# Free convolution streams, earlier key bounds and a transposed last normalization in a kernel of attention beside a long convolution

## The chip, the cores and the metric

The kernel runs on one core of a Trainium2 chip. The core has five engines with queues of their own: TensorE (matrix products into PSUM), VectorE, ScalarE, GpSimd and SyncE, which here only issues DMA transfers; GpSimd issues some too. Work passes between engines by semaphores, and each engine takes its instructions strictly in the order in which the program has them. The metric is the time of one execution on the device in microseconds (us); lower is better.

## The reference

Two independent parts stand side by side in the output (2048 rows, 576 + 576 columns).

Part A is a long convolution. For each of 576 channels a kernel K of 2048 taps is made from 128 complex modes, and the input u is convolved with it causally:

```python
dt = jnp.exp(log_dt)[:, None]
logdA = dt * (A_re + 1j * A_im)
P = jnp.exp(logdA[:, :, None] * l[None, None, :])
K = jnp.einsum("dn,dnl,dn->dl", Cc, P, dt * Bc).real
y = irfft(rfft(u, 2L) * rfft(K, 2L))[:L] + u * Dskip
```

Part B is attention with 32 query heads of width 18 that share one key head and one value head, over 2048 rows:

```python
q = (x @ wq) in 32 heads;  k = x @ wk;  v = x @ wv
p = softmax(q @ k.T * 18 ** -0.5)
out = concat_heads(p @ v) @ wo
```

## The kernel before

**Tiling of part B.** The queries are cut into four chunks c of 512 columns, the heads into 16 pairs, the keys into 16 blocks kb of 128. One *score tile* is the scores of one key block against the 512 queries of two heads (`scores`, two matmuls into one PSUM tile s of 128 x 1024). ScalarE takes the exponential of the tile into P (`exponentials`, one ACTIVATE of about 1.03 us each, 1024 of them). Then `product` multiplies the P of two score tiles (four heads, a group g) by the values and adds them in the PSUM tile o over the 16 key blocks. The value matrix carries columns of ones, so row 18 of every head's 32 rows of o holds the sum by which the head must be divided. Score tiles have three PSUM buffers (NS = 3), and the main loop goes in rounds of three: three score tiles, then products and other work until ScalarE has released the first of the three. P has ten buffers.

Before a group's scores can be made, its queries must be projected (`qproj`, matmuls q), split into two half-precision parts (qh, ql), and given a *shift row* that keeps the exponential in range. The shift comes from a bound: `settle` and `bounds` (lines 371 and 393) make for all query rows the largest key entries (kmx, a matmul into 20 columns, then kmax), and `bound` (line 504) multiplies them with the largest query entries (aw), sums with a small matmul (up), takes the running maximum (un, u) and writes the shift row (sh), which goes to DRAM by a DMA that GpSimd issues. SyncE fetches the complete operand (aug) from DRAM. No query projection but the first begins before `bounded` is set.

When a group is done, o goes to DRAM (od). `normalize` (line 577) fetches the sums, inverts them, stores them (rden), fetches them again spread over 18 rows each (db), and multiplies; `outproj` does the product with wo (op). For the last chunk three quarters of this are done in parts as the groups finish, and `finish` (line 664) does the last group after the last exponential: it inverts the sums where they lie (VectorE, two halves of 256 columns), spreads them over the rows of their head by a matmul with a 0/1 matrix b4 (bc), scales the last o, and adds the product with wo (fin) to the partial result.

**Tiling of part A.** The channels go in 12 groups k of 48. `front(k)` makes the kernel: powers and factors on VectorE and ScalarE (four groups share one set of powers, kept in DRAM), tables of products on VectorE (tab), and matmuls kg that sum the modes (`kgen`); the result ksb goes through DRAM (kd) into another layout kt. `back(k)` transforms the inputs u (matmuls hu, lu) and the kernel kt (hk, lk) by matmuls with a table of cosines and sines, multiplies the spectra on VectorE (pt, acc), and transforms back (iy). There is one buffer kt: `front(k + 1)` holds its finished kernel until `back(k)` has read the former one.

**What sets the order.** The instruction order of TensorE, ScalarE and VectorE is written out by the program itself when it is built. A planner (`main`, `Clock`, `Stream`) keeps modelled clocks of the three engines. Side work is written as generators (streams): `side` (query and output projections), `tail` (bounds), `prep` (normalization) and the convolution's streams. Each stops at points of a kind: "v" (VectorE work may follow), "p" (matmuls may follow), "b" (an activation table is wanted), "w" (it waits for another stream). In every round `fill` asks the streams for work as long as the modelled TensorE has room, and the constants RATE to C12 say how much room, how far ahead VectorE may be and which stream comes first; PLAN sets them anew in 16 stages of 32 steps (a step is two score tiles). Except for the score tiles and o, all matmuls write to one shared PSUM bank (`bank`, tile f): the next user has to wait until VectorE has emptied it.

In the convolution `turn` starts the pair `back(k)` and `front(k + 1)` and starts the next pair when both have ended; among the two, `go` asks the one first that has done less work.

Of the kernel before, what the change touches and what calls it, by code (L numbers as in the profile page):

```python
# [17 lines left out]
P = 128  # L18
# [32 lines left out]
LAST = 576.841  # L51
# [3 lines left out]
    0: dict(RATE=1.86, PACE=1.856, AHEAD=0.729, TOTAL=340.0, GAP=0.359, DEFER=0.395, SLACK=3.285, HEAD=17.08, LEFT=1.086, C1=0.549, C2=0.718, C3=0.83, C4=1.39, C5=0.739, C6=1.059, C7=0.572, C8=0.186, C9=0.382, C10=0.431, C11=24.516, C12=11.926),  # L55
    1: dict(RATE=1.838, AHEAD=0.731, HEAD=10.76, C3=0.633, C4=1.288, C6=0.962, C8=0.227, C11=22.979),
    2: dict(AHEAD=0.937, TOTAL=426.375, SLACK=2.955, HEAD=8.992, LEFT=1.137, C3=0.83, C4=1.267, C6=0.825, C11=24.516),
    3: dict(AHEAD=0.729, TOTAL=340.0, DEFER=0.389, SLACK=3.285, HEAD=13.454, LEFT=1.086, C2=0.563, C6=1.059, C8=0.186),
    4: dict(PACE=1.877, DEFER=0.395, C2=0.718, C3=0.886, C8=0.257, C12=9.229),
    5: dict(DEFER=0.334, C1=0.507, C3=0.973, C9=0.468, C10=0.418),  # L60
    6: dict(C3=0.912, C4=1.331, C5=0.562, C8=0.216, C9=0.573, C12=11.451),
    7: dict(TOTAL=393.142, HEAD=15.028, C1=0.596),
    8: dict(PACE=1.856, C8=0.186, C12=14.796),
    9: dict(GAP=0.311, DEFER=0.395, C1=0.601, C2=0.561, C6=0.861, C9=0.468),
    10: dict(PACE=1.834, HEAD=14.988, C1=0.497, C9=0.382),
    12: dict(TOTAL=300.519, C1=0.607, C2=0.687, C12=11.271),
    13: dict(AHEAD=0.591, TOTAL=393.142, SLACK=2.63, C1=0.65, C5=0.726, C6=1.059, C10=0.39, C12=14.796),
    14: dict(C1=0.533, C2=0.561, C7=0.595, C9=0.379, C12=11.755),
    15: dict(AHEAD=0.503, C3=1.026, C4=1.582, C8=0.194),
# [144 lines left out]
class Attention:  # L214
# [36 lines left out]
    def setup(self, tp, conv):  # L251
# [51 lines left out]
        self.tails = []  # L303
# [67 lines left out]
    def settle(self, conv):  # L371
# [17 lines left out]
        K.t += 1.0  # L389
        K.v = K.t + 2.0  # L390
        K.fill = K.v

    def bounds(self):

        nc, V, K = self.nc, self.V, self.k
        km, spread = self.km, self.spread
        self.bounded = True
        pk = self.bank(20, "kmx")
# [406 lines left out]
    def main(self, conv, flag):  # L805
# [75 lines left out]
        for r in range(0, len(pairs), NS):  # L881
# [22 lines left out]
            if r == 2 * NS:  # L904
                self.bounds()
# [727 lines left out]
```

## Time and profile before

| | us |
|---|---|
| median of 3 runs | 1141.29 (1140.82 to 1143.82) |
| the profiled execution | 1140.67 |
| its span, first to last instruction | 1138.9 |
| first exponential of the main loop | 26.79 |
| end of the last exponential | 1121.02 |
| busy: TensorE, VectorE, ScalarE | 1080.4, 992.7, 998.9 |

The profile names engines PE (TensorE), PEld (TensorE's weight loads), DVE (VectorE), ACT (ScalarE), POOL (GpSimd) and SP (SyncE). A row of a group or of the timeline ends, in square brackets or behind a bar, with the idle time just before it and what ended it. A row of the waits reads: who waited, for whom, total, times, longest. Row counts of fp32 matmuls are twice those of the program, since each is done in two passes. Line numbers are those of the kernel before. Vector operations of many streams share one helper line (137), so groups are told by their tiles: `out<-in`.

### The profile page before, as it was taken

The page shows a single profiled execution, that of the slowest core. Times are in us where ns is not written, and L with a number is a line of the kernel's source. Part 1 is how long each engine was busy: PE and PEld are TensorE (multiplying, and loading weights), DVE is VectorE, ACT ScalarE, POOL GpSimd, SP SyncE. Part 2 cuts the span into 40 slices and gives each one's busy share as a digit, 9 for nine tenths or more (in the row PEclk, how much of TensorE's full clock was granted, in tenths as well). Part 3 has the DMA queues.
Part 4 walks back from the last instruction along what each step waited for, and adds up shares of the span by engine and source line. Part 5 has one row for each costly group of instructions (what it writes and reads, how often), then busy time and mean ns, then how long its engine had stood idle before and what let it go on. Part 6 is the DMA issues. An engine that isn't in the chain of part 4 may idle for free.

```text
span 1138.9 us, 33011 instructions
## 1 busy us (share of the span) xinstructions
PE 1080.4 (95%) x13886; PEld 395.6 (35%) x13886; DVE 992.7 (87%) x1692; ACT 998.9 (88%) x1052; POOL 140.0 (12%) x257
## 2 busy tenths in 40 slices
PE   6999999998998999999999999999989999999997
PEld 2333333333333333323333333333322333433423
DVE  3878998899899898998799899899699799799794
ACT  2878988888997899999898999899999999889993
POOL 4442324122023000000201211000000000000000
PEclk9999999999999999999999999999999999999999
DMA  7432234212222301122202301201222311311201
GB/s 224 146 101 75 64 118 135 63 39 50 84 82 87 95 29 59 50 88 88 89 9 82 106 22 36 97 29 40 68 95 67 99 40 38 97 39 35 72 30 59
DMA packets 59279, 83.37 MB, mean 73 GB/s; under 512 B 14867, under 2 KB 35335, under 8 KB 58613
## 3 DMA queue, kind: packets, MB, share of 16 engines
q1 hardware_dynamic: 47557, 73.24, 20.1%
q0 software_dynamic: 10848, 7.37, 2.6%
q8 instruction: 111, 1.82, 0.7%
q10 hardware_dynamic: 720, 0.58, 0.2%
q14 instruction: 43, 0.35, 0.1%
HBM read 46.59 MB, written 33.85 MB: 71 GB/s over the span
## 4 chain that ended last, share of the span: by engine, by line
PE 59%; DVE 21%; ACT 10%; issue 6%; DMA 3%; POOL 1%; DVEq 0%; SPq 0%; ACTq 0%
PE ops L869 24%; PE s L550 15%; ACT P L561 9%; PE op L211 5%; DVE tab L137 5%; PE kg L1314 3%; DVE ks L137 3%; PE iy L211 3%; PE q L427 2%; DVE acc L137 2%; DVE tt L137 1%; PE hu L211 1%; PE hk L211 1%; DVE pt L137 1%; DMA db<-rden 1%
## 5 line engine op out<-in xcount | busy, mean ns | idle before, releaser
L561 ACT ACTIVATE P<-s 128x1024 f32<-128x1024 f32 x992 | 934.8, 1035 | 97.2 <-PE s L550 94.3
L869 PE MATMUL ops<-P,v_sb 128*32 128x512 f32 x4096 | 509.5, 599 | 3.0 <-DVE o L141 2.8
L550 PE MATMUL s<-aug,kaug 55*128 55x512 f16 x2048 | 307.5, 381 | 23.6 <-ACT P L561 20.8
L550 PEld LDWEIGHTS <-kaug 55*128 55x128 f16 x2048 | 93.2, 94 | 341.6 <-issue 292.9
L869 PEld LDWEIGHTS ops<-P,v_sb 128*32 128x32 f32 x4096 | 118.2, 110 | 162.8 <-issue 131.0
L478 POOL DMA_DIRECT2D qd<-qh x116 | 66.3, 578 | 317.8 <-DVE qh L145 315.2
L427 PE MATMUL q<-x,wq_sb 128*32 128x256 f32 x1360 | 83.6, 382 | 0.3 <-PE s L550 0.3
L211 PE MATMUL op<-wo_sb,oT 126*32 126x288 f32 (+1 forms) x960 | 67.5, 410 | 2.5 <-DVE ob L141 2.5
L1225 POOL MEMSET fr<- 128x192 f32 x24 | 9.9, 497 | 481.6 <-DVE tt L137 242.5
L137 DVE TENSOR_TENSOR tab<-tab,tt 128x576 f32<-128x576 f32 (+1 forms) x72 | 59.0, 820 | 1.5
L137 DVE TENSOR_TENSOR tab<-fr,dif 128x576 f32<-128x576 f32 (+1 forms) x72 | 58.7, 815 | 0.0
L137 DVE TENSOR_TENSOR tt<-fr,sum 128x576 f32<-128x576 f32 (+1 forms) x72 | 58.7, 815 | 0.0
L137 DVE TENSOR_TENSOR tab<-sum,fr 128x576 f32<-128x576 f32 (+1 forms) x72 | 58.6, 814 | 0.0
L137 DVE TENSOR_TENSOR tab<-tab 128x576 f32<-128x576 f32 (+1 forms) x72 | 58.5, 813 | 0.0
L141 DVE COPY ksb<-kg 128x192 f32<-128x192 f32 x48 | 17.3, 360 | 41.5 <-PE kg L1314 41.5
L427 PEld LDWEIGHTS q<-x,wq_sb 128*32 128x32 f32 x1360 | 39.9, 109 | 38.4 <-issue 14.4
L137 DVE TENSOR_TENSOR acc<-acc,pt 128x1728 f32<-128x1728 f32 (+2 forms) x36 | 48.6, 1349 | 0.2
L137 DVE TENSOR_TENSOR pt<-us,ks 128x1728 f32<-128x1728 f32 (+2 forms) x36 | 48.3, 1347 | 0.0
L1314 PE MATMUL kg<-tab 128*32 128x64 f32 x2304 | 41.8, 220 | 5.6 <-DVE tab L137 3.4
L1314 PEld LDWEIGHTS kg<-tab 128*32 128x32 f32 x2304 | 36.5, 110 | 29.6 <-issue 9.8
L559 ACT ACTIVATE P<-s,bias 128x1024 f32<-128x1024 f32 x32 | 33.0, 1115 | 13.4 <-PE s L550 13.4
L137 DVE TENSOR_TENSOR ks<-ks 128x576 f32<-128x576 f32 (+1 forms) x48 | 41.0, 855 | 1.0
(163 smaller groups left out, 1020.9 us busy)
## 6 DMA issues: line engine op xcount, KB each, us to landing
od<-o SPq DMA_DIRECT2D x31, 256.0 KB
aug<-qd SPq DMA_DIRECT2D x124, 55.0 KB
u<-u SPq DMA_DIRECT2D x12, 384.0 KB
kd<-ksb SPq DMA_DIRECT2D x12, 384.0 KB
kt<-kd SPq DMA_DIRECT2D x48, 96.0 KB
outa<-u SPq DMA_DIRECT2D x12, 384.0 KB
pw<-pw SPq DMA_DIRECT2D x8, 528.0 KB
db<-rden SPq DMA_DIRECT2D x16, 252.0 KB
```

Of the source, the lines that this page charges most:

```text
L137: return self.v.tensor_tensor(out, *a, **k)
L141: return self.v.tensor_copy(out, *a, **k)
L211: nc.tensor.matmul(ps[j:e], w[:, j:e], x, start=start, stop=stop, tile_position=(0, j))
L427: nc.tensor.matmul(ps[o, 256 * f:256 * f + 256], w[:, k, i], xt[:, k, x], start=(k == 0), stop=(k == 4), tile_position=(0, 32 * j))
L478: q.dma_start(qd[h:h + n, row + d:row + d + nd, cs], src[i1:i1 + n * nd, :cs.stop - cs.start])
L550: nc.tensor.matmul(ps[:, j, :], self.kaug[r, kb * P:(kb + 1) * P], t[r, :], start=True, stop=True)
L559: nc.scalar.activation(pt, ps, AF.Exp, bias=self.bias, scale=SCALE / QQ)
L561: nc.scalar.activation(pt, ps, AF.Exp, scale=SCALE / QQ)
L869: nc.tensor.matmul(o_ps[32 * j:32 * j + 32, :], self.v[:, kb, :], pts[2 * n + j // 2][:, j % 2, :], start=(kb == 0), stop=(kb == 15), tile ...
L1225: nc.gpsimd.memset(t[:, :, 0:NF:8], one)
L1314: nc.tensor.matmul(ps[32 * g:32 * g + 32, d, :], t[:, :32], t[:, 32:], start=(j == 0), stop=(j == 1), tile_position=(0, 32 * g))
```

## The change

1. **Key bounds.** What `bounds` did in the third round of scores is now done at the end of `settle`, in the first round, directly behind the matmuls that transpose the values. Its PSUM tile comes from the output pool (o) and no longer from the shared bank.
2. **Shift rows.** The tile sh has three buffers where it had one.
3. **Normalization.** While the main loop runs, the multiplication is asked for 7.0 us (model time) behind its fetch, where it was 4.6.
4. **Last sums.** `finish` copies the last o (ScalarE one half, VectorE the other), brings the 4 sums of each query to the partitions with 16 small matmuls, inverts a tile of 128 x 16, and spreads the inverses with 16 matmuls against the identity (id4, loaded behind b4).
5. **Convolution streams.** The pairs are gone. One stream runs all fronts, one all backs. A back waits until the front of its group (first group) or of the group before (all others) has sent its kernel, transforms u, and only then waits for its own kernel. Of two streams that both have VectorE work, the one served last comes first.
6. **Table.** PLAN has 32 stages of 16 steps, other values, and LAST is 618.0 where it was 576.8. The modelled cost of a round of scores is 0.04 us less.

```diff
-LAST = 576.841
+LAST = 618.01458
 PLAN = {
...
+    0: dict(RATE=1.87109, PACE=1.81374, AHEAD=0.81305, TOTAL=379.90864, GAP=0.27563, DEFER=0.50556, SLACK=3.20468, HEAD=12.56556, LEFT=0.69661, C1=0.35905, C2=0.57071, C3=0.95845, C4=1.22733, C5=0.56371, C6=0.74724, C7=0.51086, C8=0.17113, C9=0.53612, C10=0.37123, C11=37.75411, C12=17.28614),
...
+LAG = (0, -1)
@@ settle: @@
-        K.t += 1.0
-        K.v = K.t + 2.0
-        K.fill = K.v
-
-    def bounds(self):
...
         self.bounded = True
-        pk = self.bank(20, "kmx")
+        pk = self.ps_o.tile([P, CT], F32, tag="o", name="kmx")[:, :20]
...
-        K.pe(1.5)
-        K.v = max(K.v, K.t + 0.5)
-        K.fill = K.v + 0.25
+        K.t += 2.3
+        K.fill = K.t - 0.5
+        K.v = K.t + 0.7
@@ bound: @@
-        sh = self.p2.tile([8, 256], F16, tag="sh", name=f"sh{c}_{m}", bufs=1)
+        sh = self.p2.tile([8, 256], F16, tag="sh", name=f"sh{c}_{m}", bufs=3)
@@ normalize: @@
-            yield "v", max(K.t, fetched[m] + 4.6), False
+            yield "v", max(K.t, fetched[m] + (4.6 if self.over else 7.0)), False
@@ finish: @@
-        for f in range(2):
-            V.tensor_scalar(rc[:, half[f]], o_ps[:, half[f]], 1e-37, None, op0=ALU.max)
-            nc.scalar.activation(o_sb[:, half[f]], o_ps[:, half[f]], AF.Copy)
-            if f == 0:
-                V.reciprocal(rc[:, half[f]], rc[:, half[f]])
...
+        nc.scalar.activation(o_sb[:, half[0]], o_ps[:, half[0]], AF.Copy)
+        V.tensor_copy(o_sb[:, half[1]], o_ps[:, half[1]])
+        begin(0, 0, tile[0][:, 0, :])
+        begin(0, 1, tile[0][:, 1, :])
+        for t in range(4):
+            matmul4(nc, bc[:, 4 * t:4 * t + 4], o_sb[:, t * P:(t + 1) * P], b4[:, 0:P:32])
+        V.tensor_scalar(rt, bc[:, 0:16], 1e-37, None, op0=ALU.max)
+        V.reciprocal(rt, rt)
+        begin(1, 0, tile[1][:, 0, :])
+        begin(1, 1, tile[1][:, 1, :])
+        for t in range(4):
+            for j in range(4):
+                nc.tensor.matmul(bc[32 * j:32 * j + 32, t * P:(t + 1) * P], rt[:, 4 * t + j:4 * t + j + 1].broadcast_to([P, 32]), self.id4, start=True, stop=True, tile_position=(0, 32 * j))
         scale(0)
+        begin(2, 0, tile[2][:, 0, :])
+        begin(2, 1, tile[2][:, 1, :])
         end(0, 0)
         end(0, 1)
+        scale(1)
         begin(3, 0, self.ps_o.tile([P, CT], F32, tag="o", name="fin3_0"))
-        V.reciprocal(rc[:, half[1]], rc[:, half[1]])
-        nc.tensor.matmul(bc[1], b4, rc[:, half[1]], start=True, stop=True)
         end(1, 0)
         end(1, 1)
         add(0, 0)
-        scale(1)
...
@@ main: @@
-            globals().update(PLAN.get(self.step // 32, {}))
+            globals().update(PLAN.get(self.step // 16, {}))
...
-            if r == 2 * NS:
-                self.bounds()
@@ Conv.back: @@
         tt(us[:, 0:4, :], us[:, 4:8, :], us[:, 8:12, :], op=ALU.add)
+        while self.begun < k:
+            yield "w", 0.0, False
+        kt = self.kt
@@ Conv: @@
+    def fronts(self):
+        for k in range(NCK):
+            yield from self.front(k)
+
+    def backs(self):
+        for k in range(NCK):
+            while self.begun < LAG[k > 0] + k:
+                yield "w", 0.0, False
+            yield from self.back(k)
...
-    def turn(self):
-
-        if self.n < NCK and not any(st.live for st in self.streams):
-            self.n += 1
-            k = self.n
-            self.streams = [Stream(self.back(k, self.kt), self.k)] if k < NCK else []
-            if k + 1 < NCK:
-                self.streams.append(Stream(self.front(k + 1), self.k))
...
-        for st in sorted(self.streams, key=lambda st: (not st.holds, st.work)):
+        for st in sorted(self.streams, key=lambda st: (not st.holds, st.kind == "v" and st is not self.on, st.work)):
             w0, st.ahead = self.k.work, ahead
+            kind = st.kind
             if st.go(step, credit, lock):
+                if kind == "v":
+                    self.on = st
```

Here `begin(t, nh, tile)` issues the matmuls of the heads that are ready, `end(t, nh)` those of the last group, `add` the addition to the partial result and the store.

More of the change, by code (lines that the diff above doesn't have):

```diff
@@ L50 @@
 TOTAL = 340.0
-LAST = 576.841
+LAST = 618.01458
 GAP = 0.4
 PLAN = {
[L55 to L69, printed above, removed]
@@ L302, in setup @@
         self.todo, self.busy, self.group = [], False, 0
-        self.tails = []
+        self.tails, self.over = [], False
         self.side_work = Stream(self.side(), self.k, 99.0)
@@ L669, in finish @@
         o_sb = self.p2.tile([P, CT], F32, tag="o", name="o_last", bufs=1)
-        rc = self.p1.tile([P, CT], F32, tag="db", name="rc_last", bufs=2)
+        rt = self.p1.tile([P, 16], F32, tag="dn", name="r_last")
         half = [slice(f * 256, f * 256 + 256) for f in range(2)]
         cols = [slice(nh * 288, nh * 288 + 288) for nh in range(2)]
-        bc = self.bank(CT, "bc").rearrange("p (f n) -> f p n", f=2)
+        bc = self.bank(CT, "bc")
         ps = {}
@@ L773, in prepare @@
                 nc.sync.dma_start(self.b4, self.a["b4"])
+                self.id4 = self.p2.tile([P, P], F32, tag="aw", name="id4")
+                nc.sync.dma_start(self.id4, self.a["ident"])
             yield from self.normalize(c, ms)
@@ L890, in main @@
                 force(lambda: 16 * c + 2 * g + j in self.ready)
-                ss[i] = self.scores(i, c, 2 * g + j, kb, 0.34 if i == r else 0.216)
-            K.t += 0.12
+                ss[i] = self.scores(i, c, 2 * g + j, kb, 0.32 if i == r else 0.216)
+            K.t += 0.1
             for i in new:
@@ L931, in main @@
                 force(lambda: nxt in self.ready)
+        self.over = True
         while behind < len(pairs) // 2:
@@ L936, in main @@
         while True:
-            conv.turn()
             h, live = holder(), [st for st in conv.streams if st.live]
@@ L1481, in early @@
         self.load(0)
-        self.n, self.burst = -1, False
-        self.streams = [Stream(self.front(0), self.k)]
+        self.burst, self.on = False, None
+        self.streams = [Stream(self.fronts(), self.k), Stream(self.backs(), self.k)]
+    def fronts(self):
[6 more added lines that the diff above has]
+            yield from self.back(k)
     def begin(self, n):
@@ L1515, in go @@
                     st.asked = step
-                if self.beside() >= 8 or step > st.asked + 16 or self.n < 0:
+                if self.beside() >= 8 or step > st.asked + 16 or self.begun < 0:
                     st.kind, st.asked = "v", -1
-        for st in sorted(self.streams, key=lambda st: (not st.holds, st.work)):
+        for st in sorted(self.streams, key=lambda st: (not st.holds, st.kind == "v" and st is not self.on, st.work)):
             w0, st.ahead = self.k.work, ahead
+            kind = st.kind
             if st.go(step, credit, lock):
+                if kind == "v":
+                    self.on = st
                 self.work += self.k.work - w0
@@ L1528, in drain @@
     def drain(self):
-        while self.streams:
-            for st in sorted(self.streams, key=lambda st: (not st.holds, st.work)):
+        while any(st.live for st in self.streams):
+            for st in sorted(self.streams, key=lambda st: (not st.holds, st.kind == "w", st.work)):
                 if st.live:
@@ L1533, in drain @@
                     break
-            self.turn()
 def build(tc, **aps):
```

49 lines of the change are left out of this document (35 added, 14 removed).

## The prediction

> **What bounds the kernel now.** I read the page first, then the busy time by stage, then the waits, then the timeline at the places that the change touches.
>
> ```profile
> span 1138.9 us, 33011 instructions
> ...
> PE 1080.4 (95%) x13886; PEld 395.6 (35%) x13886; DVE 992.7 (87%) x1692; ACT 998.9 (88%) x1052; POOL 140.0 (12%) x257
> ...
> PE 59%; DVE 21%; ACT 10%; issue 6%; DMA 3%; POOL 1%; DVEq 0%; SPq 0%; ACTq 0%
> ```
>
> TensorE is busy nearest to always and holds most of the chain of waits, but ScalarE and VectorE stand close behind, and a fifth of the chain is VectorE. So the kernel is neither bound by one engine nor idle: it loses where two of them wait for each other. The next rows are busy time by stage: the exponential stage as a whole (from the first exponential at 26.8 to the last at 1121), and two neighbours within it.
>
> ```profile
> 26.80:1121.00 1094.20, 1050.76 (x13582) 385.14 (x13585) 975.26 (x1654) 991.55 (x1042) 128.25 (x233) 1.00 0.22 69
> ...
> 700.00:800.00 100.00, 98.04 (x1332) 36.77 (x1334) 91.53 (x150) 90.68 (x97) 0.83 (x2) 1.00 0.18 56
> 800.00:900.00 100.00, 91.94 (x1032) 30.29 (x1028) 88.64 (x143) 97.81 (x104) 1.63 (x4) 1.00 0.23 76
> ```
>
> Columns after the length: TensorE, weight loads, VectorE, ScalarE, GpSimd. In the whole stage TensorE idles 1094.2 - 1050.8 = 43.4 us, ScalarE 102.7, VectorE 118.9. TensorE's work is not reduced by this change, so 43.4 us is what a better order can win at most. The two neighbours show how it is lost: from 700 to 800 TensorE is full and ScalarE idles 9.3 us; from 800 to 900 ScalarE is full and TensorE idles 8.1. The granted clock is 1.00, so the clock is no part of it. The waits say for what TensorE, ScalarE and VectorE wait (total, times, longest):
>
> ```profile
> ACT P L561 <- PE s L550: 94.3, 171, 2.9
> DVE ksb L141 <- PE kg L1314: 41.5, 34, 2.9
> ...
> PE s L550 <- ACT P L561: 20.8, 76, 0.5
> ...
> DVE sh L145 <- DMA qd<-sh: 4.7, 3, 2.1
> ...
> PE up L211 <- DVE ql L149: 3.8, 3, 2.2
> ...
> DVE oT L137 <- DMA db<-rden: 3.1, 3, 1.4
> ```
>
> About half of TensorE's idle time (20.8) is waiting for a score tile that ScalarE has not yet released: rounds into which no side work was put. The rest are short waits for VectorE. VectorE's largest wait, 41.5 us, is for the matmuls of the kernel generation (kg), where it has nothing else in its order.
>
> **The change part by part.** The sum is made against the profiled execution, 1140.7 us (its span 1138.9 and 1.8 around it), which is 0.6 under the median of the runs, 1141.3.
>
> *Key bounds.* The twelve matmul instructions (kmx) and the two VectorE operations move from behind the third round of scores to behind the value transposes in the first, and their PSUM tile from the shared bank to the output bank.
>
> ```profile
> 26.79 9.26 ACT L559 ACTIVATE P<-s,bias 128x1024 f32<-128x1024 f32 x9 [8.09 <-PE s L550]
> ...
> 27.41 0.66 PE L378 MATMUL vp<-ident,keys 128*128 128x128 f32 x4
> 28.00 0.39 PE L550 MATMUL s<-aug,kaug 55*128 55x512 f16 x2
> ...
> 30.40 1.94 PE L869 MATMUL ops<-P,v_sb 128*32 128x512 f32 x8
> ...
> 33.62 1.27 PE L401 MATMUL kmx<-km,spread_sb 128*128 128x4 f32 x12
> ...
> 34.93 0.18 DVE L153 TENSOR_REDUCE kmax<-kmx 128x5 f32<-128x20 f32 x1 [3.79 <-PE kmx L401]
> ...
> 35.56 0.67 DVE L141 COPY fr<-pw 128x192 f32<-128x192 f32 x3
> ...
> 37.54 3.12 ACT L559 ACTIVATE P<-s,bias 128x1024 f32<-128x1024 f32 x3 [1.50 <-PE s L550]
> ...
> 59.86 5.19 ACT L559 ACTIVATE P<-s,bias 128x1024 f32<-128x1024 f32 x5 [2.00 <-PE s L550]
> ...
> 68.75 2.86 ACT L561 ACTIVATE P<-s 128x1024 f32<-128x1024 f32 x3 [2.79 <-PE s L550]
> ```
>
> The 1.27 us is spent in both kernels. At the new place it lies behind the first three exponentials, which start at 26.79 and run to 29.9 (a ninth of 9.26 each): the next score would start at 28.07 + 1.27 = 29.3 and be done at 29.7, so it costs ScalarE nothing, at worst 0.4. The first product (from 30.40) now needs the output bank free of kmx; the reduction would be done at about 29.6, so that wait is covered too, and if the cover is gone it costs the 1.27. Behind the waiting reduction VectorE queues the last powers of the convolution, whose reader (fr) starts only at 35.56. What goes: VectorE's wait of 3.79, and the pause of 1.50 in ScalarE behind kmx. All query projections, which wait for the bounds, may start some 5 us earlier (the reduction at about 29.6 instead of 34.93); the pauses of 2.00 (scores queued behind a bound that waits for ql) and 2.79 (queries forced out before the second group of heads) may shrink. Between +0.4 and -(1.50 + 2.00 + 2.79) = -6.3; since TensorE is full for most of this stretch, I take -2.5, nearer to what kmx itself leaves.
>
> *Shift rows in three buffers.* The wait of 4.7 us, in three places, goes: VectorE no longer waits until the former row has reached DRAM. TensorE had other work behind each, so between 0 and -4.7; I take a third, -1.5.
>
> *Normalization asked 7.0 instead of 4.6 us behind its fetch* (until the main loop is over). VectorE's wait of 3.1 for the fetched rows goes; the output projection starts 2.4 us later, behind queries that fill that time. Between -3.1 and +0.5; a third, -1.0.
>
> *Last sums.* Two reciprocals over 256 columns and two full-array broadcasts go; in come 32 narrow matmul instructions (sums, 4 columns), one reciprocal over 16 columns, and 32 with 128 columns.
>
> ```profile
> L211 PE MATMUL up<-sel_sb,aw 128*32 128x8 f32 (+1 forms) x320 | 6.1, 177 | 4.6 <-DVE ql L149 3.8 <-DVE ksb L141 0.6
> L1314 PE MATMUL kg<-tab 128*32 128x64 f32 x2304 | 41.8, 220 | 5.6 <-DVE tab L137 3.4 <-DVE un L153 2.2
> L211 PE MATMUL hu<-u,dft_sb 128*32 128x192 f32 x384 | 21.2, 331 | 0.4 <-DVE scu L137 0.4
> L211 PE MATMUL fin<-wo_sb,wq_sb 126*32 126x288 f32 x64 | 4.7, 408 | 0.0
> L701 DVE RECIPROCAL rc_last<-rc_last 128x256 f32<-128x256 f32 x1 | 1.8, 1753 | 0.0
> L709 PE MATMUL bc<-rc_last,b 128*128 128x256 f32 x2 | 0.7, 416 | 0.0
> ...
> 1120.00:1130.00 10.00, 10.00 (x124) 3.92 (x116) 6.14 (x10) 1.79 (x3) 0.00 (x0) 1.00 0.11 42
> ```
>
> In the last stage TensorE is busy all the time (10.00 of 10), so the reciprocals of 1.8 us lie beside its work and are no gain; only TensorE's own work counts. Out: 2 x 0.7 = 1.4. In: sums by the up row 32 x 6.1/320 = 0.6; broadcasts between kg's 41.8/2304 = 18 ns and hu's 21.2/384 = 55 ns each, in the middle 32 x 37 ns = 1.2. Together +0.4, between -0.2 and +1.0. The new chain copy, sum, reciprocal, broadcast, scale has two steps of VectorE, each beside two begun sums of TensorE (the fin row, 4.7 us for eight, so 1.2). The second constant (id4) is loaded behind b4 on SyncE's queue, into a buffer that the same last reader frees: one more issue there, and no transfer that is due behind it.
>
> [...]
>
> *Free convolution streams, and the table.* Until now the back of group k and the front of k+1 formed a pair, and the next pair began when both had ended. Now fronts and backs run as two streams, and a back may transform its inputs before its kernel is there. The table of constants moves work between steps and has no price of its own. At a turn of the pair the timeline of VectorE, and the ten turns by stage, show:
>
> ```profile
> 283.74 0.76 DVE L137 TENSOR_TENSOR tab<-tab,tt 128x576 f32<-128x576 f32 x1
> 285.50 0.36 DVE L141 COPY ksb<-kg 128x192 f32<-128x192 f32 x1 [1.00 <-PE kg L1314]
> 287.06 0.36 DVE L141 COPY ksb<-kg 128x192 f32<-128x192 f32 x1 [1.20 <-PE kg L1314]
> ...
> 281.00:296.00 15.00, 14.21 (x236) 5.28 (x228) 12.09 (x29) 12.75 (x14) 0.83 (x2) 1.00 0.60 190
> ...
> sum 156.00, PE 152.02 PEld 61.29 DVE 106.53 ACT 135.67 POOL 8.97; mean PE 15.20 PEld 6.13 DVE 10.65 ACT 13.57 POOL 0.90
> ```
>
> The back is done, the front waits for its last kg, and VectorE stands; then all transforms come together. In these 156 us VectorE is busy 68% (89% in the whole stage), and ScalarE idles 20.3, where the whole stage's rate (102.7/1094.2) would give 14.6: 5.7 us more. Transforms that lie elsewhere give these back, if they land in rounds in which TensorE waits for ScalarE. From the table I take 2.5 more: were 700 to 900 even, TensorE's 190.0 us would need, at the 2% idle of its first half, 194 us, which is 6; a table that is not made from these rows gets under half of it. Together -8.2, between -(43.4 - 5.0 already used) = -38 and +10 (the loss is that of the third rival).
>
> Sum: -2.5 - 1.5 - 1.0 + 0.4 - 8.2 = -12.8; 1140.7 - 12.8 = 1127.9, and 0.6 for the median: **1128.5**. With each of the small parts at its end and the last between -3 and -14: 1122 to 1136.
>
> **The rivals.** *More of the reservoir:* the two streams fill half of TensorE's 38 us. For it: its 20.8 us lie in 76 short waits that any matmul in stock would fill. Against: what is left in each is 0.3 us, less than one group of side work. Time: 1141.3 - 4.6 - 19 = 1118.
>
> *No change:* the order is written by a planner with fixed prices; a gap closed in one round opens in the next, since TensorE's 1050.8 us stay. For it: the waits that are named in the rows are short and scattered. Time: 1141.3 with -2 to +2: 1139 to 1143. The same time results if the freed streams stay in step anyway, because a front must hold its kernel until the back has read the former one (the change doesn't do what it says).
>
> *Slower, VectorE's neighbours:* the new order keeps VectorE on the stream that it served last, where the old one took the stream with less work done. An operation that reads its forerunner then follows it directly.
>
> ```profile
> 271.49 0.74 DVE L137 TENSOR_TENSOR tab<-tab 128x576 f32<-128x576 f32 x1
> 272.15 1.01 DVE L137 TENSOR_TENSOR w<-sv 128x384 f32<-128x384 f32 x2
> 273.09 0.74 DVE L137 TENSOR_TENSOR tab<-tab,tt 128x576 f32<-128x576 f32 x1
> ...
> 282.96 0.75 DVE L137 TENSOR_TENSOR tab<-tab 128x576 f32<-128x576 f32 x1
> ```
>
> Interleaved, the successor starts 0.07 before its forerunner's end (273.09 against 272.15 + 1.01); alone, 0.03 behind it (283.74, above, against 282.96 + 0.75): 0.1 us for each new neighbour. Some 400 of the 1692 operations would be 40 us, a third of VectorE's idle 118.9; TensorE's waits for VectorE (43.4 less 20.8 for ScalarE, about 22) would then grow by nearly half, +10, and the 8.2 would not come: 1141.3 - 4.6 + 10 = 1147. It decides from about 200 new neighbours (+5 against the -4.6 of the small parts). Against it: VectorE is the engine with the most idle time.
>
> **How the numbers follow.** Forecast 0.50 (1122 to 1136), more of the reservoir 0.17, no change 0.15, slower 0.18. A measurement of this kernel can tell about 0.3% from no change, 3.4 us. Faster is the first two and a little of the third, 0.68; same 0.14; slower 0.18. The range that holds 8 of 10 cuts a tenth at each end: 1117 to 1147.
>
> **What would show it.** Key bounds: kmx directly behind vp, the 3.79 gone, no pause of 1.50 near 37. Shift rows: no wait of sh for its DMA. Normalization: no wait of oT for db. Last sums: 17 to 18 us from the last exponential to the end, as before. Streams: hu matmuls ahead of the kd store of the same turn, and the wait for kg well under 41.5. Table: no stretch of 100 us with TensorE under 93. The forecast is wrong if TensorE's idle time in the exponential stage stays above 40 us; the third rival holds if VectorE's busy time grows by more than 20 us.

## The result, and the profile after

| | before, us | after, us |
|---|---|---|
| median, side by side | 1140.82 (9 runs) | 1134.32 (9 runs) |
| the same again, beside e17 | 1139.45 (18 runs) | 1135.40 (12 runs) |
| the profiled execution | 1140.67 | 1135.17 |
| its span | 1138.9 | 1133.4 |
| first exponential | 26.8 | 27.2 |
| exponential stage | 1094.2 | 1089.5 |
| end of the last exponential to the end | 17.9 | 16.7 |

The change makes the kernel faster, by about half a percent: the ratio of the times is 0.9949 (95% interval 0.9936 to 0.9962), and 0.9964 (0.9947 to 0.9980) in the repetition. The forecast was 1128.5, 12.8 us less than before; measured are 6.5 and 4.1 us less. The sign was right, the size a half or a third of the forecast.

The page of the kernel after, its first lines and the chain of waits by engine:

```profile
span 1133.4 us, 33135 instructions
...
PE 1076.8 (95%) x13946; PEld 392.6 (35%) x13946; DVE 993.0 (88%) x1689; ACT 999.5 (88%) x1051; POOL 140.0 (12%) x257
...
PE 69%; DVE 14%; ACT 9%; issue 4%; DMA 2%; SPq 0%; POOL 0%; ACTq 0%; DVEq 0%
```

VectorE's busy time is what it was (993.0, before 992.7), and its share of the chain fell from 21% to 14%. That fall isn't the work of the freed streams: with the old streams and the two parts that keep the order (e9, below) the share is 14% as well, and with the freed streams alone (e4) it is 25%. The busy time by stage of the kernel after (length, then TensorE, weight loads, VectorE, ScalarE, GpSimd, granted clock) shows what TensorE made of it; the first row is the whole exponential stage:

```profile
27.21:1116.67 1089.46, 1047.72 (x13574) 381.21 (x13572) 979.41 (x1655) 992.57 (x1042) 127.10 (x230) 1.00 0.23 70
700.00:800.00 100.00, 95.89 (x1268) 35.05 (x1266) 88.78 (x144) 90.87 (x98) 0.83 (x2) 0.98 0.20 63
750.00:850.00 100.00, 91.69 (x1034) 31.39 (x1030) 81.30 (x128) 94.14 (x100) 0.81 (x2) 0.98 0.22 69
...
800.00:900.00 100.00, 90.10 (x962) 27.68 (x963) 85.60 (x147) 98.50 (x104) 1.61 (x4) 1.00 0.21 67
...
1027.00:1117.00 90.00, 88.99 (x1064) 31.33 (x1064) 57.51 (x94) 83.36 (x89) 0.00 (x0) 1.00 0.12 41
```

TensorE idles 1089.46 - 1047.72 = 41.7 us, where it was 43.4. The unevenness has moved, and is not gone: from 800 to 900 ScalarE is full and TensorE idles 9.9 us (before 8.1), and from 1027 on TensorE is full while ScalarE idles 6.6 us. The waits of the kernel after (who waited, for whom, total, times, longest):

```profile
ACT P L571 <- PE s L560: 91.0, 184, 3.0
...
PE s L560 <- ACT P L571: 19.6, 63, 0.5
...
DVE part L155 <- PE op L229: 13.6, 8, 2.6
DVE ksb L159 <- PE kg L1324: 13.5, 17, 1.4
DVE sck L159 <- PE hk L229: 12.3, 12, 2.3
...
DVE u L155 <- PE iy L229: 9.5, 10, 3.1
```

VectorE's wait for kg fell from 41.5 to 13.5 us. Waits for the other matmuls (op, hk, iy) stand in its place: added over all rows, VectorE waits 109.2 us for matmuls in the kernel before and 104.4 in the kernel after. TensorE's wait for ScalarE is 19.6 where it was 20.8. No shift row waits for its DMA any more, and no oT for db. The timeline of the kernel after, around the key bounds:

```profile
27.21 3.12 ACT L569 ACTIVATE P<-s,bias 128x1024 f32<-128x1024 f32 x3 [9.10 <-PE s L560]
...
28.37 1.27 PE L411 MATMUL kmx<-km,spread_sb 128*128 128x4 f32 x12 [0.22 <-DVE km L163]
29.57 1.93 PE L437 MATMUL q<-x,wq_sb 128*32 128x256 f32 x32
29.69 0.18 DVE L171 TENSOR_REDUCE kmax<-kmx 128x5 f32<-128x20 f32 x1 [0.95 <-PE kmx L411]
...
31.87 6.17 ACT L569 ACTIVATE P<-s,bias 128x1024 f32<-128x1024 f32 x6 [1.54 <-PE s L560]
```

The reduction comes at 29.69 instead of 34.93 and waits 0.95 instead of 3.79. The pause of 1.50 at 37.54 is gone, but a pause of 1.54 stands at 31.87: the planner now puts 32 query matmuls (1.93 us) ahead of the next scores, since they are allowed earlier.

Where the time went is best seen in when the n-th of the 1024 exponentials starts, after minus before: -4.6 us at number 64, -6.8 at 320, -0.9 at 640, -0.2 at 896, -4.4 at the last. Some 7 us are won in the first third, given back by number 896, and 4 are won again at the end. The rest, 1.1, is the tail.

### The profile page after: what moved, and what is told of

Read it like the earlier page. It is cut to its first block, busy times and chain, and to the rows that moved or that the text cites. A ratio compares the mean times of both kernels' runs of the same rounds, so it can differ in the third digit from the quotient of the medians.

```text
span 1133.4 us, 33135 instructions
## 1 busy us (share of the span) xinstructions
PE 1076.8 (95%) x13946; PEld 392.6 (35%) x13946; DVE 993.0 (88%) x1689; ACT 999.5 (88%) x1051; POOL 140.0 (12%) x257
## 4 chain that ended last, share of the span: by engine, by line
PE 69%; DVE 14%; ACT 9%; issue 4%; DMA 2%; SPq 0%; POOL 0%; ACTq 0%; DVEq 0%
PE ops L881 29%; PE s L560 18%; ACT P L571 9%; PE q L437 6%; PE op L229 5%; PE iy L229 3%; PE kg L1324 3%; DVE tab L155 2%; DVE acc L155 2%; PE hu L229 2%; DVE ks L155 1%; PE hk L229 1%; PE lk L229 1%; DMA xr<-xT 1%; PE lu L229 1%
## 5 line engine op out<-in xcount | busy, mean ns | idle before, releaser
L560 PE MATMUL s<-aug,kaug 55*128 55x512 f16 x2048 | 303.9, 381 | 21.8 <-ACT P L571 19.6
L437 PEld LDWEIGHTS q<-x,wq_sb 128*32 128x32 f32 x1360 | 38.6, 109 | 38.5 <-issue 16.7
L1324 PE MATMUL kg<-tab 128*32 128x64 f32 x2304 | 41.7, 220 | 0.8 <-DVE tab L155 0.3
L229 PE MATMUL iy<-w,dft_sb 128*32 128x192 f32 x768 | 37.0, 329 | 1.4 <-DVE ob L159 1.2
```

The source lines that it names most:

```text
L229: nc.tensor.matmul(ps[j:e], w[:, j:e], x, start=start, stop=stop, tile_position=(0, j))
L437: nc.tensor.matmul(ps[o, 256 * f:256 * f + 256], w[:, k, i], xt[:, k, x], start=(k == 0), stop=(k == 4), tile_position=(0, 32 * j))
L560: nc.tensor.matmul(ps[:, j, :], self.kaug[r, kb * P:(kb + 1) * P], t[r, :], start=True, stop=True)
L1324: nc.tensor.matmul(ps[32 * g:32 * g + 32, d, :], t[:, :32], t[:, 32:], start=(j == 0), stop=(j == 1), tile_position=(0, 32 * g))
```

## The experiments

Two theories stood against each other. **Theory A:** each part of the change has a price of its own, and the prices add. **Theory B:** the parts act through the instruction order that the planner writes, and what they do there isn't a price but a new order, better or worse by more than the part itself. The prediction was built on A. Three buffers for the shift rows and the new last sums leave the written order of the exponential stage exactly as it was: in the traces of before, e1, e2 and e9 the instructions of TensorE, VectorE and ScalarE come in the same sequence up to the last exponential. The bounds, the margin (the 7.0 us of the normalization), the streams and the table rewrite it from the first place that they touch.

The results together. Each ratio is against the kernel before on the same chip in the same hours; the microseconds are (ratio - 1) x 1139.4, the median of all 107 runs of the kernel before.

| run | ratio | interval | us |
|---|---|---|---|
| e1 before + shift rows | 0.9968 | 0.9954 to 0.9982 | -3.6 |
| e2 before + last sums | 0.9992 | 0.9976 to 1.0008 | -0.9 |
| e9 before + rows + sums | 0.9965 | 0.9952 to 0.9979 | -4.0 |
| e17 before + rows + sums + bounds, order held | 0.9935 | 0.9913 to 0.9958 | -7.4 |
| e3 before + margin | 1.0124 | 1.0104 to 1.0144 | +14.1 |
| e5 before + bounds | 1.0131 | 1.0096 to 1.0166 | +14.9 |
| e4 before + streams | 1.0200 | 1.0179 to 1.0221 | +22.8 |
| e6 before + table | 1.0294 | 1.0251 to 1.0337 | +33.5 |
| e10 before + margin + rows | 1.0035 | 1.0016 to 1.0054 | +4.0 |
| e15 before + streams + rows | 1.0185 | 1.0152 to 1.0217 | +21.1 |
| e16 before + bounds + rows | 1.0111 | 1.0080 to 1.0142 | +12.6 |
| e7 after, old table | 1.0080 | 1.0051 to 1.0108 | +9.1 |
| e8 after, old pairs | 1.0240 | 1.0199 to 1.0281 | +27.3 |
| e11 after, table shaken by 1% | 1.0033 | 1.0011 to 1.0054 | +3.8 |
| e12 after, old table to step 160 | 1.0076 | 1.0051 to 1.0100 | +8.7 |
| e13 after, one row buffer | 0.9978 | 0.9963 to 0.9992 | -2.5 |
| e14 after, one row buffer, old sums | 0.9983 | 0.9966 to 0.9999 | -1.9 |
| after | 0.9949 | 0.9936 to 0.9962 | -5.8 |
| e18 after, beside e17 | 0.9964 | 0.9947 to 0.9980 | -4.1 |

And the lag of the n-th exponential against the kernel before, in us, one profiled execution each, so that single entries carry about 2 us of scatter:

```
n      after     e1     e9    e17     e3    e10     e5     e4     e6     e7    e12     e8    e14
0       +0.4   -0.1   -0.8   -1.4   -0.7   -1.4   -0.6   -1.0   -1.4   -2.1   -1.0   -1.2   -1.0
64      -4.6   -1.3   -0.1   -5.3   +3.5   -3.6   -6.4   -1.0   -1.0   -7.8   -6.7   -6.1   -6.0
160     -3.9   -1.4   -0.0   -6.3   +3.5   -4.6   -6.4   +0.3   +3.9   -8.3   -7.5   -3.7   -1.9
320     -6.8   -4.0   -2.3   -6.6   +5.6   -9.9   -6.8   -3.4   +7.8  -14.4  -15.2   -8.6   -6.3
480     -2.5   -4.0   -2.3   -6.6  +11.8   -4.0   -2.6   -1.6  +11.7   -9.3   -4.9   -2.5   -2.0
640     -0.9   -4.3   -2.5   -6.3  +14.4   +0.4   -1.5   +2.4  +19.6   -4.8   +2.1   +4.8   -0.4
800     -2.0   -4.3   -2.5   -4.7  +12.9   -1.0   +9.8  +13.4  +21.3   +6.7   +7.0  +14.4   -0.1
960     -2.2   -4.3   -2.4   -4.7  +13.8   -0.1  +11.9  +18.2  +27.4   +5.3   +9.2  +16.6   -0.3
1023    -4.4   -4.3   -2.4   -4.7  +14.6   +0.7  +13.6  +17.5  +30.6   +4.6   +6.4  +17.3   -2.5
```

### The two parts that keep the order

e1, three buffers for the shift rows:

```diff
-        sh = self.p2.tile([8, 256], F16, tag="sh", name=f"sh{c}_{m}", bufs=1)
+        sh = self.p2.tile([8, 256], F16, tag="sh", name=f"sh{c}_{m}", bufs=3)
```

> The kernel before with three buffers for the shift row and nothing else; the instruction order of every engine stays the same. Theory A (the parts have prices of their own): the three waits of VectorE for the row's DMA (4.7 us) go and the time falls by about 1.5 us, between 0 and 4.7. Theory B (the parts act through the order that the planner writes; what does not change the order moves little): the waits go, the time falls by less than 1 us.

Measured: -3.6 us, more than either theory's figure and inside A's bounds. The lag shows where: in steps at the three places of the wait (-1.3 by 64, -2.5 at 224, between -4.0 and -4.4 from 288 on), and then it stays. Here a lead that is won without changing the order is kept to the end.

e2, the new `finish` and the constant id4 in the kernel before, of which this is the core:

```diff
-        rc = self.p1.tile([P, CT], F32, tag="db", name="rc_last", bufs=2)
+        rt = self.p1.tile([P, 16], F32, tag="dn", name="r_last")
```

> The kernel before with the new last sums (transposed, identity matmuls, second constant) and nothing else; the order up to the last exponential stays the same. My forecast had +0.4 us. The trace of after has 16.7 us from the last exponential's end to the end of the span, against 17.9 before. Theory A: -1.1 us, all of it behind the last exponential. Theory B, for this part, the same: no order is changed ahead of it.

Measured: -0.9 us, with an interval that holds zero. In the profile the time behind the last exponential is 16.6 us, where it was 17.9.

e9, both diffs in the kernel before:

> The kernel before with the two parts that leave the written order of the exponential stage as it was: three buffers for the shift rows, and the new last sums. If parts that keep the order keep a price of their own, the prices that they had alone add: 3.1 + 0.9 = 4.0 us less than the kernel before (2.5 to 5.5), which is most of the whole change's 6.5; the lag of the exponentials against the kernel before is that of the shift rows alone (about 4 us at the end), and the tail is 16.5 us. If even these two don't add (they wait for the same engine, or the measurement of one was scatter), 1 to 2 us less.

Measured: -4.0 us. The two prices, 3.6 and 0.9, add within their intervals, and these two small parts alone bring most of what the whole change brings.

### Each of the other parts alone

e3, the margin of 7.0 (and the flag `over`) alone:

```diff
-            yield "v", max(K.t, fetched[m] + 4.6), False
+            yield "v", max(K.t, fetched[m] + (4.6 if self.over else 7.0)), False
```

> The kernel before with the normalization asked 7.0 instead of 4.6 us behind its fetch and nothing else. Theory A: the wait of 3.1 us for the fetched rows goes, -1.0 us, and at most -3.1. Theory B: this small edit writes another order from its first use on, so the time goes anywhere between -5 and +5 us, and not with the 3.1 us of the wait.

e4, the class of the convolution streams alone:

```diff
-        self.streams = [Stream(self.front(0), self.k)]
+        self.streams = [Stream(self.fronts(), self.k), Stream(self.backs(), self.k)]
```

> The kernel before with the free convolution streams and the table of before. Theory A: VectorE's wait for kg falls from 41.5 us to about 14, as in the trace of after, and the time falls by about 5.7 us, as forecast from the turns. Theory B: the wait for kg falls just the same, since the streams do that, but the time does not follow: between -3 and +6 us, because the table's constants were made for the pairs and TensorE's idle time stays at 42 to 45 us.

e5, the bounds moved into `settle`, with their modelled costs:

```diff
-            if r == 2 * NS:
-                self.bounds()
```

> The kernel before with the key bounds moved behind the value transposes and nothing else. Theory A (prices of their own): the first 96 score tiles come out 3 to 4 us earlier, as they do in after (5.1 us, of which 1.3 belong to the shift rows), and keep that to the end: -2 to -5 us. Theory B (the order is written anew from the first round on): the start wins the same 3 to 4 us, and the end lies anywhere between -10 and +20 us, as the margin (+14) and the streams (+22) did.

e6, the table, LAST and the modelled cost of a round:

```diff
-LAST = 576.841
+LAST = 618.01458
```

> The kernel before with the table of 32 stages, its LAST and the modelled cost of a round, and nothing else: the pairs of streams and all else stay. Theory A: the table moves work between steps whatever the streams, -2.5 us. Theory B: the table is made for the order of the other parts, and without them it is as bad as the streams are without it: +5 to +25 us.

Measured: +14.1, +22.8, +14.9 and +33.5 us. Added, that would be 85 us more than before for the four parts; together they are a small gain. So Theory A is out for these parts. Theory B, by which these times don't follow the prices of the parts, fits, but its sizes were too small: it had allowed -5 to +5 us for the margin, -3 to +6 for the streams and +5 to +25 for the table; only the bounds lie in its range. The margin shows how an order loses. The timeline of e3, around its longest stall:

```profile
342.97 0.28 DVE L145 TENSOR_SCALAR sh<-u 8x256 f16<-8x256 f32 x1
...
349.24 2.34 POOL L478 DMA_DIRECT2D qd<-ql  x4 [3.10 <-DVE u L137]
351.57 0.57 POOL L530 DMA_DIRECT2D qd<-sh  x1
354.57 0.28 DVE L145 TENSOR_SCALAR sh<-u 8x256 f16<-8x256 f32 x1 [5.79 <-DMA qd<-sh]
...
360.72 1.94 PE L869 MATMUL ops<-P,v_sb 128*32 128x512 f32 x8 [3.61 <-DVE o L141]
363.30 2.85 ACT L561 ACTIVATE P<-s 128x1024 f32<-128x1024 f32 x3 [7.73 <-PE s L550]
365.35 0.34 PEld L869 LDWEIGHTS ops<-P,v_sb 128*32 128x32 f32 x8
365.56 1.03 PE L869 MATMUL ops<-P,v_sb 128*32 128x512 f32 x8
```

In this order two shift rows follow each other within 6 us. The transfer of the first is issued only at 351.57, behind GpSimd's issues of the query rows (qd<-qh, qd<-ql) and 3.10 us in which GpSimd itself waited for VectorE, so the second waits 5.79 us for the one buffer. VectorE's copy of the output bank (o) is queued behind it and behind what has gathered by then, TensorE waits for that copy, and ScalarE stands for 7.73 us.

### The whole change without one part, and the table shaken

e7, the kernel after with the old table, LAST and round cost; and e8, the kernel after with the old pairs of streams:

```diff
-            globals().update(PLAN.get(self.step // 16, {}))
+            globals().update(PLAN.get(self.step // 32, {}))
```

```diff
-        self.streams = [Stream(self.fronts(), self.k), Stream(self.backs(), self.k)]
+        self.streams = [Stream(self.front(0), self.k)]
```

> The kernel after with the table of before. Theory A (sum of the parts): -6.5 us for all less the table's 2.5, so about 4 us under before. Theory B: +10 to +30 us over before, nearer to the streams alone (+22) than to after.

> The kernel after with the pairs of streams of before, its own table kept. Theory A: the streams are worth about 5.7 us, so this lies about 1 us under before and VectorE's wait for kg is back at about 41 us. Theory B: the wait for kg is back all the same, and the time is 5 to 25 us over before, because the table was made for the free streams.

Measured: +9.1 and +27.3 us against before, so that taking the table out of the kernel after costs some 15 us and taking the streams out some 33, although either alone makes the kernel before slower. Both lie just outside what Theory B had said (+10 to +30, and 5 to 25). The timeline of e8 has another stall of the same kind, without any shift row in it:

```profile
877.00 3.64 PE L880 MATMUL ops<-P,v_sb 128*32 128x512 f32 x16 [7.01 <-DVE o L158]
...
881.28 2.86 ACT L570 ACTIVATE P<-s 128x1024 f32<-128x1024 f32 x3 [9.21 <-PE s L559]
```

e11, every constant of the new table multiplied by a random number within 1% of one (one line of it, the new values in words):

```diff
-    1: dict(AHEAD=0.61191, HEAD=16.3668, C5=0.77482, C10=0.45189),
+    1: dict(each value x (1 + a random number between -0.01 and 0.01)),
```

> The kernel after, each constant of its table multiplied by a number drawn between 0.99 and 1.01; no mechanism is touched. Theory A, by which the table has a price by what its constants mean: within 3 us of the kernel after (1131 to 1138). Theory B, by which the time hangs on the one order that just this table writes: 5 to 25 us more than the kernel after (1140 to 1160), with the loss in two or three single stalls and not spread.

Measured: +3.8 us against before, 9.6 more than the kernel after (7.9 against its repetition). A table whose values mean the same to within 1% gives away the whole gain: this is Theory B, from one draw of the numbers. By its trace it lies 3.7 us behind the kernel after at exponential 416, 1.4 ahead at 640, 5.2 behind at the last one, and its tail is 2.3 longer; the loss in two or three single stalls that Theory B had expected is not shown.

e12, the old table for the first 160 steps (exponential 320), the new one, in full, from there (the new line in words):

```diff
-    10: dict(C1=0.29902, C2=0.47216, C4=1.15188),
+    10: dict(all 21 constants as the new table has them at this stage, and the new LAST and round cost),
```

> The kernel after, with the old table (and its modelled cost of a round) for the first 160 steps and the new one from there. With the old table throughout, the exponential number 320, which is step 160, came 14.4 us ahead of the kernel before, against 6.8 in the kernel after. If a lead that has been won is kept, the time is 7 us under the kernel after (about 1127). By Theory B the lead is borrowed or the new table does not fit the state that it takes over: the lead melts behind step 160 and the time is between the kernel after and 20 us more (1134 to 1155).

Measured: +8.7 us. The lead at 320 is there (-15.2, even more than in e7), and by 640 it is +2.1. So the lead melts, as Theory B had it; whether it was borrowed or the new table doesn't fit the state that it takes over, this run doesn't tell. The leads of e1 and e17, won with the order kept, stay to within 2 us.

### Was it the one buffer?

e10, e15 and e16 put the three buffers under the margin, the streams and the bounds; the orders are those of e3, e4 and e5.

> The kernel before with the margin of 7.0 us and three buffers for the shift rows; the instruction order is the same as that of the margin alone, which took 14.3 us more than before. If the margin alone lost its time because a shift row had to wait 5.79 us for the transfer of the row before it, that wait and the stall of 7.73 us of ScalarE at 363 are gone, and the loss falls to 8 us or less (by 6 or more). If the order itself is the worse one, the stall stays in another form or the gain is the 3 us that the buffers brought in the old order: loss 11 us.

> The kernel before with the free streams and three buffers for the shift rows; the instruction order is the same as that of the streams alone, which took 22 us more than the kernel before and waited 6.5 us for shift rows in three places (longest 3.1). If the one buffer made the loss, as with the margin: it falls by 8 us or more, to 14 or less. If the order made it: it falls by 3 to 6 us, about what the waits are long, and 16 to 19 us remain.

> The kernel before with the moved bounds and three buffers for the shift rows; the order is that of the bounds alone, which took 14.9 us more than the kernel before and waited 4.0 us for shift rows in three places (longest 2.0). If the one buffer made the loss: it falls by 8 us or more, to 7 or less. If the order made it: it falls by 2 to 4 us, and 11 to 13 remain.

Measured: the buffers win back 10.1 us of 14.1 for the margin, but 1.7 of 22.8 for the streams and 2.3 of 14.9 for the bounds, less than even the smaller of the two expected amounts for the streams. For the margin the one buffer made most of the loss; for the other two it did not. Their loss lies in the order, and late: the lags of e4 and e5 run away between 640 and 800. Which decision of the planner starts it stays open.

e13 and e14 take the order-keeping parts out of the kernel after (e13 keeps its order; in e14 only the end differs, where the former `finish` stands again):

```diff
-        sh = self.p2.tile([8, 256], F16, tag="sh", name=f"sh{c}_{m}", bufs=3)
+        sh = self.p2.tile([8, 256], F16, tag="sh", name=f"sh{c}_{m}", bufs=1)
```

> The kernel after with one buffer for the shift rows; the written order is that of the kernel after. If the buffers have the price that they had in the order before: 3 to 4 us more than the kernel after, 1137 to 1138. If what a buffer is worth hangs on the order, as under the margin where it was 10: 6 to 12 us more (1140 to 1146), with waits of a shift row for its transfer of 3 us and longer. If the new order, written with its table by this very planner, has spread the rows so that one buffer is enough: nothing.

> The kernel after with one buffer for the shift rows and the former last sums: what is left of the change are the four parts that rewrite the order (bounds, margin, streams, table). If the two order-keeping parts carry most of the gain: 4 us or more over the kernel after, 1138 or more, so that the four others together lie within 2 us of the kernel before or above it. If the four others carry it by themselves: within 2 us of the kernel after (1133 to 1136).

Measured: -2.5 and -1.9 us against before. The two parts are worth 3.9 us in the kernel after (2.2 against its repetition), the row buffers 1.6 to 3.3 of it (without them the rows wait 2.9 us for their transfer in the profile of e13). What is left of the change, the four parts that rewrite the order, is -1.9 us, with an interval from -3.9 to -0.1. And -1.9 with the -4.0 of e9 is -5.9, which is the -5.8 of the whole change (-4.1 in the repetition).

### The bounds in the old order

e17 takes e9 and puts the twelve kmx matmul instructions and their two VectorE operations behind the value transposes, as in the kernel after, but restores the planner's clocks behind them and leaves the flag `bounded` and the modelled costs at the old place:

```diff
+        clock = dict(K.__dict__)
+        pk = self.ps_o.tile([P, CT], F32, tag="o", name="kmx")[:, :20]
...
+        K.__dict__.update(clock)
```

> The kernel before with three buffers for the shift rows, the new last sums, and the twelve kmx matmul instructions with their two VectorE operations put behind the value transposes, as in the kernel after, but with the planner's clocks and the point from which projections may begin left as they were: nothing else in the written order changes. If the moved bounds have a price of their own (the pause of ScalarE for kmx, 1.5 us in the kernel before and 4.8 in the run with rows and sums): 1.5 to 5 us less than rows and sums alone, a ratio of 0.991 to 0.995 against the kernel before, as fast as the kernel after or faster. If the pause only moves to the next tile that waits (the queries behind it): no difference from rows and sums, 0.9965.

> The kernel after once more, on the chip of the run beside it: a ratio of 0.9949 again, within 0.0013. If the old order with three parts has the lower time, the four rewritten parts of the change brought nothing that the old order could not have had.

Measured: 1132.47 us, a ratio of 0.9935; the kernel after beside it 1135.40. The difference of the two means is 2.7 us, give or take 1.6: the old order with three small edits is faster than the kernel after. Some 1 us of the 2.7 goes with the granted clock, 0.9961 on average over the runs of e17 and 0.9948 over those beside it, if 0.001 of it is worth 0.7 to 1.0 us as in the other runs on this chip. The kernel after missed its expectation by a little: 0.9964, where 0.9936 to 0.9962 was said. The bounds are worth some 3 us here (0.9965 to 0.9935; the intervals of the two overlap slightly, so the size is rough). The timeline of e17 at the place:

```profile
26.71 1.17 PE L393 MATMUL kmx<-km,spread_sb 128*128 128x4 f32 x12
27.93 0.18 DVE L153 TENSOR_REDUCE kmax<-kmx 128x5 f32<-128x20 f32 x1 [0.48 <-PE kmx L393]
...
34.94 3.12 ACT L568 ACTIVATE P<-s,bias 128x1024 f32<-128x1024 f32 x3 [0.26 <-PE s L559]
```

The pause before these exponentials is 0.26 us; it was 1.50 in the kernel before, and 4.84 in the profile of e9, whose TensorE ran at half clock just then, from 29.9 to 40.1 us: the twelve kmx rows take 2.18 us there, 1.17 in e17:

```profile
32.80 2.18 PE L401 MATMUL kmx<-km,spread_sb 128*128 128x4 f32 x12
35.03 0.18 DVE L153 TENSOR_REDUCE kmax<-kmx 128x5 f32<-128x20 f32 x1 [4.97 <-PE kmx L401]
...
39.99 3.13 ACT L559 ACTIVATE P<-s,bias 128x1024 f32<-128x1024 f32 x3 [4.84 <-PE s L550]
```

Here the pause does not move to the next tile, because no query was allowed to jump ahead.

## Why the prediction was half right

**Key bounds, -2.5.** kmx stands directly behind vp, and the 3.79 is gone, as forecast. With the order held the edit brought about 3 us (e17), so the mechanism was right, and the size as far as it can be told. As the change makes it, with `bounded` set earlier, it rewrites the order: +14.9 us alone. The step "all query projections may start some 5 us earlier; the pauses of 2.00 and 2.79 may shrink" was counted as a gain only.

**Shift rows, -1.5.** The wait went, and with it 3.6 us of the 4.7, not a third. The step that was off is "TensorE had other work behind each": it was taken to cover two thirds of the wait. Mechanism right, size off by two.

**Normalization, -1.0.** Wrong in sign for the part alone: +14.1, and still +7.6 with three buffers on both sides (e10 against e1). The wait of 3.1 is gone in e3, and the forecast left out what the later multiplication does to the rest of the order and to the one row buffer. Where the other 7.6 us come from stays open.

**Last sums, +0.4.** Measured -0.9 (interval -2.7 to +0.9), and 0.6 when taken out of the kernel after. The group of the broadcasts after, and of the sums:

```profile
L719 PE MATMUL bc<-id,r_last 128*32 128x128 f32 x32 | 1.1, 273 | 0.0
...
L229 PE MATMUL bc<-b,o_last 128*32 128x4 f32 x32 | 0.5, 175 | 0.0
```

The two terms came out as worked out (1.1 for 1.2, 0.5 for 0.6). The tail is 16.7 us, where 17 to 18 was forecast. The interval holds the +0.4 too, so these runs don't decide the sign.

**Streams and table, -8.2.** This is the step that failed. What it said of the trace came true: hu runs ahead of the kd store of the same turn (270.52 and 284.73 us), and the wait for kg fell to 13.5. But "transforms that lie elsewhere give these back" took idle time of ScalarE in ten turns for time of the kernel, and "were 700 to 900 even" took a table for something that evens out (TensorE's 190.0 us of work in these 200 are 186.0 in the kernel after, and 800 to 900 is less even than before). VectorE's wait for kg was not what ended the time. The kg waits of e9 and e4, and the group of the same copies in e17, show it:

```profile
DVE ksb L141 <- PE kg L1316: 41.3, 32, 2.9
...
DVE ksb L142 <- PE kg L1314: 20.2, 20, 2.4
...
L141 DVE COPY ksb<-kg 128x192 f32<-128x192 f32 x48 | 17.3, 360 | 44.0 <-PE kg L1325 43.9
```

With the wait as long as before, e9 is 4.0 us faster; with the wait halved, e4 is 22.8 slower. And e17, the fastest kernel of all, waits 43.9 us. In the kernel after, what VectorE no longer waits for kg it waits for other matmuls (109.2 us in all before, 104.4 after), and TensorE's 43.4 idle us became 41.7. All four parts that rewrite the order, priced at -2.5 - 1.0 - 8.2 = -11.7, are together -1.9 (e14). The two that keep it, priced at -1.1, are -4.0 (e9). The forecast's own tests said so: TensorE's idle time stayed above 40, and there are stretches of 100 us with TensorE under 93 (91.69, 90.10).

**The rivals.** VectorE's neighbours are out: its busy time rose by 0.3 us, not by 20. More of the reservoir is out: TensorE still idles 41.7 us. "No change" was right in its mechanism for the four rewriting parts (a gap closed in one round opens in the next), and wrong in its time because of the two parts that don't touch the order.

**The range and the clock.** The measured times lie inside 1122 to 1136, which is luck in part: the four rewriting parts brought 9.8 us less than their price and the two others 2.9 more, and the range doesn't follow from its own terms. With the small parts at the ends that are named and the last at -3 or -14, the sum runs from -28.3 to -1.1, 1113 to 1140. The clock was put at nothing from a rounded 1.00; up to the last exponential the profile of before has three stretches of 3.4 us at half clock and that of after two, at half of the difference an effect of 1.7 us at most; it is told below.

What is shown: the sizes of the parts with the order kept, and that the rewriting parts, as the change makes them, have no prices that add (85 us more alone, 1.9 less together). What is argued only: that the new table was fitted to the other parts; e6, e7 and e11 are what one would see then. No run tries another table for the freed streams, so what they could bring at best stays open.

## What to carry to other kernels

Where a planner writes the instruction order, separate edits that keep the order (compare the two orders first) from edits that rewrite it. The first can be priced from the waits in the profile, and here their prices added within the intervals and their lead was kept; the second are a new draw, here 14 to 34 us worse for each alone, and one 1% shake of the constants cost more than the whole change brings. So try an edit with the order held first: three of them in the old order (e17) beat the change with its new planner.

## What was not expected of the hardware

TensorE's clock falls to half in the middle of a kernel that keeps it 95% busy. In the kernel after, the granted clock is 0.50 from 793.9 to 797.3 us, for 3.4 us; the busy time there, in stretches of the same length, shows it (length, TensorE, weight loads, VectorE, ScalarE, GpSimd, granted clock):

```profile
787.10:790.50 3.40, 3.23 (x30) 0.72 (x22) 3.40 (x5) 3.40 (x5) 0.00 (x0) 1.00 0.60 153
790.50:793.90 3.40, 1.32 (x10) 0.30 (x6) 3.33 (x5) 3.40 (x5) 0.00 (x0) 1.00 0.09 27
793.90:797.30 3.40, 2.85 (x24) 0.99 (x24) 1.39 (x2) 2.28 (x2) 0.00 (x0) 0.50 0.21 77
797.30:800.70 3.40, 3.02 (x48) 1.27 (x44) 1.58 (x3) 2.72 (x3) 0.00 (x0) 1.00 0.27 76
```

Behind a stretch in which TensorE was busy for 1.32 of 3.40 us, the next runs at 0.50. The timeline of the same place: an output product of 8 matmul rows takes 1.94 us there and 1.04 just before.

```profile
787.58 1.04 PE L881 MATMUL ops<-P,v_sb 128*32 128x512 f32 x8
...
794.45 1.94 PE L881 MATMUL ops<-P,v_sb 128*32 128x512 f32 x8 [1.98 <-DVE o L159]
```

So, as an estimate from these rows, the wait of 1.98 us may have cost up to 1.7 more (half of the 3.40 at 0.50); that the wait brought the lower clock isn't shown. Two other stretches of this trace in a row, from 107.9 to 114.7, are busy for 1.72 and 1.70 of 3.40 us, and the clock stays at 1.00; in the kernel before, one with 1.63 (344.1 to 347.5) is followed by a clock of 0.51, and one with 2.22 (26.7 to 30.1) by 0.50. So the busy time just before doesn't tell whether the clock falls, and these traces don't show what does.

Up to the last exponential the kernels before and after have three and two such stretches in their profiles (from 30.1, 135.9 and 347.6 us, and from 326.3 and 793.9; 10.2 and 6.8 us at half clock), the slow variants e3 to e6 20 to 27 us, e8 34 (mean granted clock of the profiled executions 0.994 and 0.996, 0.988 to 0.990, and 0.984). At half of that, 10 to 17 us lost against 3 to 5 would be a good part of what a worse order costs, but this is an upper bound and no run isolates it: e9 and e17 have 17.1 and 13.7 us at half clock and are faster than the kernel before, and e9, with 10.2 of them between 29.9 and 40.1 us, is 0.1 us ahead of the kernel before at exponential 64. The scatter between runs of one kernel goes with the clock too: over the first 9 runs of the kernel after, 0.92 us for each 0.001 of mean granted clock (correlation -0.96); the other sets of at least 9 runs give 0.4 to 1.0, with weaker correlations.
